# Attention's two banks of a score tile told apart, TensorE's branch hint moved, weight conversions spread again, two penalties on VectorE

## The chip, the cores and the metric

One core of a Trainium2 chip runs the whole program in one launch. The metric is the device time of that core in microseconds (us), lower is better. TensorE (PE) multiplies, ScalarE (ACT), VectorE (DVE) and GpSimd (POOL) work on tiles in SBUF and PSUM, and SyncE (SP) issues most DMAs.

## The reference

Three layers follow one another on 4 x 576 tokens of 512 features.

```python
# attention, 4 batches x 8 heads x 576 x 64
scores = scale * np.matmul(q, k.transpose(0, 1, 3, 2))
kth = np.partition(scores, -32, axis=-1)[..., -32:-31]
scores = np.where(scores >= kth, scores, -1e9)
attn = softmax(scores); out = attn @ v
# experts: each token goes to the one expert of 8 whose normalised embedding is nearest
for e in range(8):
    h = np.maximum(x[mask] @ w1[e], 0.0)
    out[mask] = gate_w[mask, None] * (h @ w2[e])
# last two layers: 512 -> 2048 -> 512
h = x @ w_in
g = np.maximum(h, 0.0) + alpha * np.minimum(h, 0.0)
out = g @ w_out
```

w_in and w_out come as float64, so that each half of one of their units has to be turned from pairs of 32-bit words into floats.

## The kernel before

**Attention.** A tile is 128 queries of a pair of heads; there are nine for each pair and sixteen pairs. Nothing reorders instructions: each engine runs them as the code writes them, and a tile framework adds the waits between engines from the overlaps of what they read and write. The loop `tiles` walks over the tiles with a lag of its own for each stage. For every tile PE makes scores (L189, tile s), ACT copies them (L201, tile ss), DVE finds the 32nd largest (L211 to L224, then L233 and L234 with the help of ACT's sign, L286, and POOL's product, L297), ACT takes exponentials (L291, tile e), and a penalty (tile pen, 1 where a key is to be dropped) is made. The penalty has three makers, and `kind` chooses: 0 is one operation on DVE (L240), 1 one on ACT, 2 three on POOL (nk, mg, pen: L304 to L306). PE transposes e and adds the penalty times minus 2^100 (L322, L323), ACT's Relu brings the result to SBUF (pT, L342, and for the last rows of two tiles pb, L345), and PE multiplies it with the values (L356, L359).

A score tile s is two PSUM banks. When a tile's scores have been copied, their space is lent out: bank 0 holds pt1, the transposed last keys of two tiles, which ACT reads as pb. Bank 1 (`spare_psum`) holds work of the router, which picks the experts and runs between the tiles of the next batch: transposes (L646), dot products (L662, L666) and counts (L716 to L720), read by DVE (tT L653, own L735). The framework orders accesses to one tile, so that pb waits for the router's matmuls written before it, and the router's copies wait for pb.

**Experts.** Nine blocks of tokens go through the experts, two of expert 0 and one for each other, in order of their counts. In a block `blocks` makes eight hidden pieces f (PE; ACT's L1290 and DVE's L1291 evacuate them as hT) and four output pieces dc (y, L1342 and L1344). I number the blocks i = 0 to 8. After each piece `tick` does a share of the block's `plan`: plan[2i] goes with the hidden pieces of block i, plan[2i+1] with its output pieces. An item of a plan is a 512 KB load into one of four buffers raw (SP, L940 or L1000) and, later, its conversion: of an expert's weights one operation each on ACT (L1066) and on DVE or POOL (L1067); a `wide` item, half a unit of w_in or w_out, takes four on DVE (L878, L879, L880, L882) and one on POOL (wf, L1004). Sixteen wide items are dealt out over m entries of the plan from entry `first` on, with `WIDE = (first, m)`. Loads go out three items ahead, and each waits for its buffer.

The width of a block is chosen at run time: `columns_of` writes a piece twice, under a branch on PE. After block 1 one large branch ("narrow") picks one of three written versions of all that follows; a hint for its prefetch stands ahead of it.

**Last layers.** 18 groups k of 256 tokens, nine for each half of the features. For each, PE makes eight features f (L1144 to L1146) and seven products m of group k-1 (L1477, Strassen's scheme), in the order of `MIXED`: f0 f1 1 f2 f3 6 f4 7 f5 5 f6 f7 4 2 3. Each feature or product takes one of six PSUM banks in turn. DVE adds products up (y, L1478), finishes features (L1413) and makes the sums for the scheme (L1434 to L1437); ACT and POOL split operands of products (hT, L1429 and L1430). `weights(k, f)` calls `tick` for the other sixteen wide items in groups 0 to 7; that of (7, 7) converts the last one.

Of the kernel before, what the change touches and what calls it, by code (L numbers as in the profile page):

```python
# [21 lines left out]
P = 128  # L22
# [26 lines left out]
class Attention:  # L49
# [374 lines left out]
    def tiles(self, jobs, first, pair_done, batch_done, drain):  # L424
# [31 lines left out]
        for i in range(-1, n + 9):  # L456
# [6 lines left out]
            self.spare = None  # L463
# [58 lines left out]
class Router:  # L522
# [106 lines left out]
    def pair_done(self, b, hp, mx):  # L629
# [14 lines left out]
        def turn_tail():  # L644
            st["t"] = self.att.spare_psum(P)
            nc.tensor.transpose(st["t"][:D, :P], mx, self.ident)  # L646
        ready = [("wait", lambda: self.routed == b)] if hp == 0 else []
        if b == B - 1 and hp == NPAIR - 1:
# [4 lines left out]
            ("late", lambda: nc.vector.tensor_copy(self.tT[:, hp, :, :TAIL],  # L653
                                                     st["t"][:D, :P].rearrange("p (h t) -> p h t", h=2))),
            lambda: setattr(self, "turned", (b, hp))]

    def dots(self, p, t):

        mm = self.nc.tensor.matmul
# [24 lines left out]
    def batch_done(self, b):  # L684
# [25 lines left out]
        def counts():  # L710
            if b == B - 1:
                p = st["c"] = self.att.ps.tile([P, 4, P], F32, name="pt0", bufs=2).rearrange("p a b -> p (a b)")
            else:
                p = st["c"] = self.att.spare_psum((n + 1) * E)
            for t, (k, _) in enumerate(xs):
                nc.tensor.matmul(p[:, t * E:(t + 1) * E], self.tri[:k], ohb[:k, t], start=True, stop=(t == 0))  # L716
                for u in range(t):
                    nc.tensor.matmul(p[:, t * E:(t + 1) * E], self.ones, ohb[:, u], start=False, stop=(u == t - 1))
            for t, (k, _) in enumerate(xs):
                nc.tensor.matmul(p[:, n * E:(n + 1) * E], self.ones[:k], ohb[:k, t], start=(t == 0), stop=(t == n - 1))  # L720

        def place():
            v.tensor_tensor(off, st["c"][:, :n * E].rearrange("p (a b) -> p a b", b=E), be(self.run), op=OP.add)
            v.tensor_tensor(self.run, self.run, st["c"][:, n * E:(n + 1) * E], op=OP.add)
# [8 lines left out]
        def tile_copy(t):  # L733
            k = xs[t][0]
            v.tensor_copy(lg[:k, t], st[t][:k, k:k + E])  # L735

        def tile_norm(t):
            p, k = st[t], xs[t][0]
            d = wk.tile([P, P], F32, name="diag", bufs=1)
            v.scalar_tensor_tensor(d[:k, :k], p[:k, :k], 1.0, self.ident[:k, :k], op0=OP.mult, op1=OP.mult,  # L740
                                   accum_out=ss[:k, t:t + 1])
# [152 lines left out]
WIDE = (2, 12)  # L894
# [10 lines left out]
class Experts:  # L905
# [271 lines left out]
    def columns_of(self, less, products, whole=False):  # L1177
# [87 lines left out]
    def blocks(self, blocks, plan, which, xT, rows, caps=None):  # L1265
# [7 lines left out]
        for i in which:  # L1273
# [45 lines left out]

            def turn(at):  # L1320
# [4 lines left out]
            for dc in range(4):  # L1325
                if i == 1 and dc == 2:
                    self.tc.mark_branch_hint_location("narrow", "LikelyTaken", ENGINES)
                ps = self.bank()[:, :n]
                for fs in (range(4), range(4, 8)):
# [6 lines left out]
                    self.columns_of(less, products)  # L1336
# [42 lines left out]
    def last_products(self, t, n0, n1):  # L1379
# [158 lines left out]
        for k in range(last + 1):  # L1538
# [3 lines left out]
            for s in order:  # L1542
# [47 lines left out]
                weights(k, f)  # L1590
# [380 lines left out]
```

## Time and profile before

| what | value |
|---|---|
| median of 3 runs (lowest to highest) | 1100.07 us (1098.76 to 1100.5) |
| the profiled execution, its own time | 1102.43 us |
| span of its trace | 1100.6 us |
| PE, DVE, POOL, ACT busy | 96%, 80%, 68%, 66% of the span |
| mean granted clock of PE | 0.992 |

The shares are over the whole span; attention (0 to about 460 us), the experts (to 703.5 us) and the last layers have different bounds, so each is read by itself. An idle time with its releaser (the event that ended it) stands in square brackets in a timeline. Granted clock 1.00 is 2.4 GHz, 0.50 is 1.2 GHz.

### The profile page before, as it was taken

The page shows a single profiled execution, that of the slowest core. Times are in us where ns is not written, and L with a number is a line of the kernel's source. Part 1 is how long each engine was busy: PE and PEld are TensorE (multiplying, and loading weights), DVE is VectorE, ACT ScalarE, POOL GpSimd, SP SyncE. Part 2 cuts the span into 40 slices and gives each one's busy share as a digit, 9 for nine tenths or more (in the row PEclk, how much of TensorE's full clock was granted, in tenths as well). Part 3 has the DMA queues.
Part 4 walks back from the last instruction along what each step waited for, and adds up shares of the span by engine and source line. Part 5 has one row for each costly group of instructions (what it writes and reads, how often), then busy time and mean ns, then how long its engine had stood idle before and what let it go on. Part 6 is the DMA issues. An engine that isn't in the chain of part 4 may idle for free. (4 is left out here: it accounts for less than half of the span.)

```text
span 1100.6 us, 27595 instructions
## 1 busy us (share of the span) xinstructions
PE 1057.3 (96%) x9521; PEld 1004.6 (91%) x9521; DVE 877.0 (80%) x3462; ACT 723.5 (66%) x1546; POOL 745.6 (68%) x788
## 2 busy tenths in 40 slices
PE   5999999999999998999999999999999999999996
PEld 4888889888988897999999999999999999999996
DVE  6999999999999999767676675688899988466555
ACT  6999999999999999735445556454334355433441
POOL 6999999888888888424435544255656685664674
PEclk9999999999999999999999999999999999999998
DMA  7565433343343324267757686137656122212301
GB/s 176 133 154 147 105 96 95 104 124 100 91 109 98 73 65 166 57 206 227 233 195 246 224 268 213 38 96 105 127 119 113 40 63 92 78 58 72 120 22 40
DMA packets 149266, 134.49 MB, mean 122 GB/s; under 512 B 94942, under 2 KB 117470, under 8 KB 149110
## 3 DMA queue, kind: packets, MB, share of 16 engines
q1 hardware_dynamic: 145062, 122.39, 41.0%
q0 software_dynamic: 2912, 9.46, 2.4%
q8 instruction: 85, 1.39, 0.6%
q10 hardware_dynamic: 1136, 0.67, 0.2%
q14 instruction: 71, 0.58, 0.2%
HBM read 89.49 MB, written 33.63 MB: 112 GB/s over the span
## 5 line engine op out<-in xcount | busy, mean ns | idle before, releaser
L1144 PE MATMUL mm<-xT,wt 128*128 128x256 f32 (+7 forms) x852 | 243.1, 285 | 1.6 <-DVE y L1478 1.4
L1145 PE MATMUL mm<-xT,wt 128*128 128x256 f32 (+7 forms) x852 | 243.4, 286 | 0.0
L1146 PE MATMUL mm<-xT,wt 128*128 128x256 f32 (+7 forms) x852 | 242.7, 285 | 0.0
L297 POOL TENSOR_TENSOR sg<-ss,sg 128x576 f32<-128x576 f32 x143 | 201.7, 1413 | 32.3 <-ACT sg L286 30.6
L211 DVE MAX8 cand<-ss 128x8 f32<-128x96 f32 x864 | 210.2, 244 | 8.6 <-ACT ss L201 7.9
L1477 PE MATMUL mm<-wt,hT 128*128 128x256 f32 x1512 | 193.4, 282 | 0.3 <-POOL hT L1430 0.2
L1477 PEld LDWEIGHTS mm<-wt,hT 128*128 128x128 f32 x1512 | 184.9, 189 | 1.2 <-POOL hT L1430 0.6
L1144 PEld LDWEIGHTS mm<-xT,wt 128*128 128x128 f32 x852 | 160.6, 189 | 2.4 <-DVE y L1478 2.1
L1145 PEld LDWEIGHTS mm<-xT,wt 128*128 128x128 f32 x852 | 160.9, 189 | 0.5 <-DVE xT L1375 0.2
L1146 PEld LDWEIGHTS mm<-xT,wt 128*128 128x128 f32 x852 | 160.8, 189 | 0.0
L1004 POOL TENSOR_TENSOR wf<-wa,raw 128x512 f32<-128x512 f32 x32 | 44.9, 1403 | 112.5 <-DVE raw L882 84.2
L286 ACT ACTIVATE sg<-ss,w 128x576 f32<-128x576 f32 x144 | 118.4, 822 | 4.0 <-DVE w L224 3.5
L291 ACT ACTIVATE e<-ss,sm 128x576 f32<-128x576 f32 x144 | 117.7, 817 | 0.0
L322 PE MATMUL pt<-ident,e 128*128 128x128 f32 x576 | 116.3, 282 | 0.3 <-ACT pT L342 0.2
L323 PE MATMUL pt<-away,pen 128*128 128x128 bf16 x576 | 107.4, 222 | 2.7 <-POOL pen L306 2.7
L233 DVE MAX8 w<-sg 128x8 f32<-128x576 f32 x144 | 106.5, 739 | 0.0
L189 PE MATMUL s<-kt,qq 64*128 64x144 f32 (+1 forms) x1280 | 100.9, 311 | 5.2 <-ACT pb L345 2.3
L201 ACT ACTIVATE ss<-s 128x576 f32<-128x576 f32 x144 | 100.2, 696 | 5.4 <-PE s L189 3.4
L1067 POOL TENSOR_TENSOR wt<-raw,wt 128x1024 fp32r<-128x1024 f32 x28 | 70.0, 2502 | 47.7 <-ACT wt L1066 44.8
L189 PEld LDWEIGHTS s<-kt,qq 64*128 64x128 f32 (+1 forms) x1280 | 79.4, 184 | 22.1 <-issue 8.2
L356 PE MATMUL po<-va,pT 128*128 128x65 f32 (+1 forms) x640 | 86.6, 278 | 6.6 <-ACT pc L391 5.9
L342 ACT ACTIVATE pT<-pt 128x512 f32<-128x512 f32 x144 | 91.8, 637 | 1.6 <-PE pt L323 1.6
(301 smaller groups left out, 2729.2 us busy)
## 6 DMA issues: line engine op xcount, KB each, us to landing
raw<-in_moe_w SPq DMA_DIRECT2D x59, 512.0 KB
xr<-yt SPq DMA_DIRECT2D x17, 512.0 KB
qq<-qt SPq DMA_DIRECT2D x60, 144.0 KB
xs<-zeros SPq DMA_DIRECT2D x8, 1028.0 KB
raw<-in_moe_w_in SPq DMA_DIRECT2D x16, 512.0 KB
raw<-in_moe_w_out SPq DMA_DIRECT2D x16, 512.0 KB
yt<-zeros SPq DMA_DIRECT2D x8, 704.0 KB
rows<-in_q SPq DMA_DIRECT2D x32, 144.0 KB
```

Of the source, the lines that this page charges most:

```text
L189: nc.tensor.matmul(s[to, g, c * n:c * n + n], t["qq"][of, h, q0:q0 + m], t["k"][of, h * HALF + c * n:h * HALF + c * n + n], start=True, st ...
L211: blocks.append(lambda i=i: nc.vector.max(A.cand[:, i], A.ss[:, i * BW:(i + 1) * BW if i + 1 < KB else S]))
L233: fin = [lambda: nc.vector.max(C.w[:, 24:32], C.z), lambda: nc.vector.scalar_tensor_tensor(scr, self.vsel, C.c1, C.w[:, 23:32, None].to_br ...
L286: nc.scalar.activation(T.sg, T.ss, AF.Sign, bias=T.w[:, 23:24], scale=-ABOVE, accum_out=T.c1)
L291: nc.scalar.activation(T.e[:, self.place(T)], T.ss, AF.Exp, bias=T.sm[:, 0:1], scale=0.125)
L297: eng.tensor_tensor(T.z, T.ss, T.sg, op=OP.mult)
L322: nc.tensor.matmul(o, T.e[:, k:k + P], self.ident, is_transpose=True, start=True, stop=False)
L323: nc.tensor.matmul(o, T.pen[:, k:k + P], self.away, start=False, stop=True)
L1144: nc.tensor.matmul(ps, wh, xh, start=first, stop=False)
L1145: nc.tensor.matmul(ps, wh, xl, start=False, stop=False)
L1146: nc.tensor.matmul(ps, wl, xh, start=False, stop=last)
L1477: nc.tensor.matmul(ps, a[:, x, c], b[:, y, c], start=c == r == 0, stop=c == 3 and r == 2)
```

## The change

Five edits in one:

1. `kind` returns 0 for the first two tiles: their penalties are made by one operation each on DVE, not by three on POOL.
2. `other_columns` notes the router's accesses to bank 1 of a score tile, and `st_evac_a` declares that ACT's pb (bank 0) does not depend on them, nor they on it. In the last batch (where `tail` is set) nothing changes.
3. PE's hint for "narrow" moves to both sides of a branch one piece of block 1 earlier; that of the other engines stays.
4. `WIDE` goes from (2, 12) to (2, 14): the sixteen wide items lie on plan[2] to plan[15], not plan[2] to plan[13]. By entry they were 1,1,2,1,1,2,1,1,2,1,1,2 and become 1,1,1,1,1,1,2,1,1,1,1,1,1,2. Loads in blocks 2 to 7: before 12, 11, 10, 11, 11, 8; now 11, 10, 11, 10, 10, 11.
5. In `last_products` the weights of (7, 7) are called after products 4, 2 and 3 of that group, not before them.

```diff
     def kind(self, T):
+        if T.n < 2:
+            return 0
...
+    def other_columns(self, x):
+
+        if self.tail is None:
+            if self.piece is not None:
+                self.tc.declare_no_dep(x.ins, self.piece.ins, reason="other columns")
+            self.aside.append(x)
+        return x
...
-            nc.scalar.activation(T.both, T.pt1, AF.Relu)
+            x = nc.scalar.activation(T.both, T.pt1, AF.Relu)
+            if self.tail is None:
+                self.piece = x
+                for a in self.aside:
+                    self.tc.declare_no_dep(x.ins, a.ins, reason="other columns")
...
-            self.spare = None
+            self.spare, self.aside, self.piece = None, [], None
...
-        mm = self.nc.tensor.matmul
+        mm = lambda *a, **k: self.att.other_columns(self.nc.tensor.matmul(*a, **k))
...
-WIDE = (2, 12)
+WIDE = (2, 14)
...
         with self.tc.If(self.room > self.at) as wide:
+            hint()
             products(0)
         with wide.Else():
+            hint()
             products(less)
...
-                    self.tc.mark_branch_hint_location("narrow", "LikelyTaken", ENGINES)
+                    self.tc.mark_branch_hint_location("narrow", "LikelyTaken", ENGINES[1:])
...
-                    self.columns_of(less, products)
+                    self.columns_of(less, products, hint=near if i == 1 and dc == 1 and fs[0] else lambda: None)
...
-                weights(k, f)
+                if (k, f) != (ng - 2, 7):
+                    weights(k, f)
+            if k == ng - 2:
+                weights(k, 7)
```

The same wrapper goes around the router's other matmuls, transposes and copies (L646, L653, L716 to L724, L735, L740).

Three places in the order of the instructions, all on DVE. The first is near the start: ss_125 and ss_129 are the scores of the second and the sixth tile, the row with kth makes the threshold of the second. Before:

```order
L226 TENSOR_TENSOR sm<-w,own 128x4
L234 SCALAR_TENSOR_TENSOR scr,kth<-own,c_318,w 128x18
L600 TENSOR_SCALAR en<-en 8x1
L601 RECIPROCAL en<-en 8x1
L211 MAX cand<-ss_129 128x8
```

And now (the first tile's penalty stands 17 rows earlier, behind the threshold of that tile):

```order
L226 TENSOR_TENSOR sm<-w,own 128x4
L234 SCALAR_TENSOR_TENSOR scr,kth<-own,c_318,w 128x18
L614 TENSOR_SCALAR en<-en 8x1
L615 RECIPROCAL en<-en 8x1
L240 TENSOR_SCALAR pen_133<-ss_125,kth 128x576
L211 MAX cand<-ss_129 128x8
```

One operation over 576 columns has come in ahead of the sixth tile's maxima. The second place is the end of the hidden pieces of block 5 (280 columns wide), on the version of the program that ran. Before:

```order
L1067 TENSOR_TENSOR wt_27248<-raw_9002,wt_27248 128x1024
L1181 UNCONDITIONAL_BRANCH
L1291 SCALAR_TENSOR_TENSOR hT<-mm_8878,hT 128x280
L1291 SCALAR_TENSOR_TENSOR hT<-mm_8877,hT 128x280
L878 TENSOR_SCALAR wa<-raw_9103 128x512
L879 SCALAR_TENSOR_TENSOR wa<-raw_9103,wa 128x512
L880 TENSOR_SCALAR raw_9103<-wa 128x512
L882 SCALAR_TENSOR_TENSOR raw_9103<-raw_9103 128x512
L1291 SCALAR_TENSOR_TENSOR hT<-mm_8874,hT 128x280
L1291 SCALAR_TENSOR_TENSOR hT<-mm_8875,hT 128x280
```

And now:

```order
L1083 TENSOR_TENSOR wt_27263<-raw_8874,wt_27263 128x1024
L1309 SCALAR_TENSOR_TENSOR hT<-mm_8869,hT 128x280
L1309 SCALAR_TENSOR_TENSOR hT<-mm_8866,hT 128x280
L1309 SCALAR_TENSOR_TENSOR hT<-mm_8867,hT 128x280
L1083 TENSOR_TENSOR wt_27356<-raw_9095,wt_27356 128x1024
```

The second wide conversion, four operations, no longer stands ahead of the last two hidden pieces. The third place is the turn from group 7 to group 8 in the last layers: y are the sums of products 4, 2 and 3, the row behind them (L1413) finishes the first feature of group 8. Before:

```order
L1434 TENSOR_TENSOR wt_28682<-wt_28682 128x4x128
L1436 TENSOR_TENSOR wa<-wt_28682 128x512
L1437 TENSOR_TENSOR wt_28682<-wt_28682,wa 128x4x128
L878 TENSOR_SCALAR wa<-raw_8882 128x512
L879 SCALAR_TENSOR_TENSOR wa<-raw_8882,wa 128x512
L880 TENSOR_SCALAR raw_8882<-wa 128x512
L882 SCALAR_TENSOR_TENSOR raw_8882<-raw_8882 128x512
L1478 TENSOR_TENSOR y<-mm_8876,y 128x256
L1478 TENSOR_TENSOR y<-mm_8873,y 128x256
L1478 TENSOR_TENSOR y<-mm_8878,y 128x256
L1413 SCALAR_TENSOR_TENSOR xr_8495<-xr_8495,alpha,mm_8877 128x256
L1022 TENSOR_TENSOR raw_9002<-wf 128x1024
```

And now:

```order
L1458 TENSOR_TENSOR wt_28675<-wt_28675,wa 128x4x128
L1499 TENSOR_TENSOR y<-mm_8868,y 128x256
L1499 TENSOR_TENSOR y<-mm_8865,y 128x256
L1499 TENSOR_TENSOR y<-mm_8870,y 128x256
L894 TENSOR_SCALAR wa<-raw_8874 128x512
L895 SCALAR_TENSOR_TENSOR wa<-raw_8874,wa 128x512
L896 TENSOR_SCALAR raw_8874<-wa 128x512
L898 SCALAR_TENSOR_TENSOR raw_8874<-raw_8874 128x512
L1434 SCALAR_TENSOR_TENSOR xr_8487<-xr_8487,alpha,mm_8869 128x256
L1038 TENSOR_TENSOR raw_8994<-wf 128x1024
```

The three sums now stand ahead of the conversion. On POOL the order at this place is the same before and now: the conversion's wf, then the split hT that reads the sum wa of L1436 and is an operand of product 6.

## Rows read from the trace of the kernel before

**Rows 1.** Attention: length, PE, PEld, DVE, ACT, POOL busy, granted clock, DMA, GB/s.

```profile
40.00:160.00 120.00, 115.08 (x1208) 101.68 (x1206) 112.25 (x723) 119.52 (x269) 112.01 (x143) 1.00 0.46 117
160.00:180.00 20.00, 20.00 (x212) 18.59 (x211) 18.49 (x122) 18.52 (x42) 17.71 (x25) 1.00 0.49 125
```

**Rows 2.** ACT's waits for POOL, 20 to 40 us: total us, times, longest.

```profile
ACT ss L201 <- POOL mg L305: 1.4, 2, 0.8
```

**Rows 3.** DVE's timeline at the start: start, us, instruction, [idle before, releaser].

```profile
22.49 0.14 DVE L600 TENSOR_SCALAR en<-en 8x1 f32<-8x1 f32 x1 [0.60 <-POOL en L599]
...
25.89 0.50 DVE L240 TENSOR_SCALAR pen<-ss,kth 128x576 bf16<-128x576 f32 x1
```

**Rows 4.** ACT's only idle time between 33 and 156 us, from its timeline.

```profile
33.58 0.78 ACT L286 ACTIVATE sg<-ss,w 128x576 f32<-128x576 f32 x1 [0.16 <-DVE w L224]
```

**Rows 5.** ACT's waits before pb over the span: us in total, times, longest.

```profile
ACT pb L345 <- PE s L662: 2.4, 6, 0.5
...
ACT pb L345 <- PE s L666: 2.0, 3, 0.7
...
ACT pb L345 <- PE s L720: 0.7, 3, 0.2
```

**Rows 6.** DVE's timeline late in the router's first stretch.

```profile
189.22 0.28 DVE L653 COPY tT<-s 64x128 f32<-64x128 f32 x1 [0.51 <-ACT pb L345]
```

**Rows 7.** ACT's timeline behind it.

```profile
192.88 0.78 ACT L286 ACTIVATE sg<-ss,w 128x576 f32<-128x576 f32 x1 [0.71 <-DVE w L224]
```

**Rows 8.** PE's timeline, its first idle time after 150 us.

```profile
195.96 1.30 PE L189 MATMUL s<-kt,qq 64*128 64x144 f32 x16 [0.45 <-ACT pb L345]
```

**Rows 9.** PE's timeline, the first instruction behind the "narrow" branch.

```profile
510.40 0.34 PE L1144 MATMUL mm<-xT,wt 128*128 128x400 f32 x1
```

**Rows 10.** The experts' blocks 4 to 8, columns as in Rows 1.

```profile
578.87:606.07 27.20, 27.20 (x206) 27.20 (x205) 17.50 (x26) 14.86 (x25) 14.28 (x8) 1.00 0.72 233
606.07:634.38 28.31, 26.26 (x203) 25.84 (x201) 17.87 (x30) 14.09 (x24) 14.63 (x8) 0.94 0.72 235
634.38:658.44 24.06, 23.53 (x202) 23.04 (x201) 17.82 (x25) 12.54 (x23) 12.20 (x7) 1.00 0.80 264
658.44:681.89 23.45, 23.00 (x202) 22.62 (x201) 12.87 (x24) 14.05 (x25) 13.34 (x6) 1.00 0.82 261
681.89:703.48 21.59, 21.59 (x194) 21.59 (x193) 14.87 (x21) 10.70 (x20) 4.80 (x2) 1.00 0.09 29
```

**Rows 11.** DVE's timeline in block 5's hidden pieces.

```profile
614.27 0.43 DVE L878 TENSOR_SCALAR wa<-raw 128x512 int32<-128x512 int32 x1 [2.75 <-DMA raw<-in_moe_w_out]
...
619.73 0.41 DVE L878 TENSOR_SCALAR wa<-raw 128x512 int32<-128x512 int32 x1
...
621.97 0.80 DVE L1291 SCALAR_TENSOR_TENSOR hT<-mm,hT 128x280 fp32r<-128x280 f32 x2
```

**Rows 12.** PE's timeline at the same place.

```profile
622.47 0.39 PE L1145 MATMUL mm<-hT,wt 128*128 128x264 f32 x1 [1.98 <-DVE hT L1291]
```

**Rows 13.** The stretches behind that wait, columns as in Rows 1.

```profile
622.40:624.40 2.00, 1.93 (x10) 1.93 (x11) 2.00 (x3) 0.38 (x1) 2.00 (x2) 0.64 0.25 86
624.40:626.40 2.00, 2.00 (x11) 2.00 (x11) 1.15 (x4) 1.33 (x2) 2.00 (x1) 0.51 0.72 254
```

**Rows 14.** DVE's timeline at the turn from group 7 to group 8.

```profile
868.35 0.42 DVE L878 TENSOR_SCALAR wa<-raw 128x512 int32<-128x512 int32 x1
...
870.60 1.08 DVE L1478 TENSOR_TENSOR y<-mm,y 128x256 f32<-128x256 f32 x3
```

**Rows 15.** PE's timeline there, feature 2.

```profile
871.07 0.39 PE L1144 MATMUL mm<-xT,wt 128*128 128x256 f32 x1 [1.13 <-DVE y L1478]
```

**Rows 16.** PE's timeline there, product 6.

```profile
874.01 1.84 PE L1477 MATMUL mm<-wt,hT 128*128 128x256 f32 x12
```

**Rows 17.** POOL's timeline there.

```profile
870.77 1.31 POOL L1004 TENSOR_TENSOR wf<-wa,raw 128x512 f32<-128x512 f32 x1 [5.85 <-DVE raw L882]
872.03 2.33 POOL L1430 TENSOR_TENSOR hT<-wa,hT 128x512 fp32r<-128x512 f32 x1
```

More of the change, by code (lines that the diff above doesn't have):

```diff
@@ L645, in turn_tail @@
             st["t"] = self.att.spare_psum(P)
-            nc.tensor.transpose(st["t"][:D, :P], mx, self.ident)
+            self.att.other_columns(nc.tensor.transpose(st["t"][:D, :P], mx, self.ident))
         ready = [("wait", lambda: self.routed == b)] if hp == 0 else []
@@ L652, in pair_done @@
             ("st_sign2", lambda: nc.scalar.activation(self.xT[:, hp, :, :P], st["p"], AF.Copy)),
-            ("late", lambda: nc.vector.tensor_copy(self.tT[:, hp, :, :TAIL],
-                                                     st["t"][:D, :P].rearrange("p (h t) -> p h t", h=2))),
+            ("late", lambda: self.att.other_columns(nc.vector.tensor_copy(
+                self.tT[:, hp, :, :TAIL], st["t"][:D, :P].rearrange("p (h t) -> p h t", h=2)))),
             lambda: setattr(self, "turned", (b, hp))]
     def dots(self, p, t):
-        mm = self.nc.tensor.matmul
+        mm = lambda *a, **k: self.att.other_columns(self.nc.tensor.matmul(*a, **k))
         for c in range(4):
@@ L710, in counts @@
         def counts():
+            mm = lambda *a, **k: self.att.other_columns(nc.tensor.matmul(*a, **k))
             if b == B - 1:
@@ L715, in counts @@
             for t, (k, _) in enumerate(xs):
-                nc.tensor.matmul(p[:, t * E:(t + 1) * E], self.tri[:k], ohb[:k, t], start=True, stop=(t == 0))
+                mm(p[:, t * E:(t + 1) * E], self.tri[:k], ohb[:k, t], start=True, stop=(t == 0))
                 for u in range(t):
-                    nc.tensor.matmul(p[:, t * E:(t + 1) * E], self.ones, ohb[:, u], start=False, stop=(u == t - 1))
+                    mm(p[:, t * E:(t + 1) * E], self.ones, ohb[:, u], start=False, stop=(u == t - 1))
             for t, (k, _) in enumerate(xs):
-                nc.tensor.matmul(p[:, n * E:(n + 1) * E], self.ones[:k], ohb[:k, t], start=(t == 0), stop=(t == n - 1))
+                mm(p[:, n * E:(n + 1) * E], self.ones[:k], ohb[:k, t], start=(t == 0), stop=(t == n - 1))
         def place():
-            v.tensor_tensor(off, st["c"][:, :n * E].rearrange("p (a b) -> p a b", b=E), be(self.run), op=OP.add)
-            v.tensor_tensor(self.run, self.run, st["c"][:, n * E:(n + 1) * E], op=OP.add)
+            free = self.att.other_columns
+            free(v.tensor_tensor(off, st["c"][:, :n * E].rearrange("p (a b) -> p a b", b=E), be(self.run), op=OP.add))
+            free(v.tensor_tensor(self.run, self.run, st["c"][:, n * E:(n + 1) * E], op=OP.add))
         nc.vector.memset(lg[:, 4], 1.0)
@@ L734, in tile_copy @@
             k = xs[t][0]
-            v.tensor_copy(lg[:k, t], st[t][:k, k:k + E])
+            self.att.other_columns(v.tensor_copy(lg[:k, t], st[t][:k, k:k + E]))
         def tile_norm(t):
@@ L739, in tile_norm @@
             d = wk.tile([P, P], F32, name="diag", bufs=1)
-            v.scalar_tensor_tensor(d[:k, :k], p[:k, :k], 1.0, self.ident[:k, :k], op0=OP.mult, op1=OP.mult,
-                                   accum_out=ss[:k, t:t + 1])
+            self.att.other_columns(v.scalar_tensor_tensor(d[:k, :k], p[:k, :k], 1.0, self.ident[:k, :k], op0=OP.mult,
+                                                          op1=OP.mult, accum_out=ss[:k, t:t + 1]))
         def last_copies():
@@ L1175, in bank, with columns_of @@
         return self.mm[(0, 5, 4, 1, 2, 3)[self.used % 6]]
-    def columns_of(self, less, products, whole=False):
+    def columns_of(self, less, products, whole=False, hint=lambda: None):
         if less == 0 or whole:
@@ L1318, in blocks, with near @@
             self.n = len(plan[2 * i + 1])
+            def near():
+                self.tc.mark_branch_hint_location("narrow", "LikelyTaken", ENGINES[:1])
             def turn(at):
```

## The prediction

> **What bounds the kernel now.** I began with the view that gives each engine's busy time by stretch, since the three layers have different limits. In plain attention ACT is busy 119.52 of 120 us and PE 115.08: ACT sets the pace, PE has little to spare. Where the router's dots run, PE is busy 20.00 of 20 and ACT only 18.52: there PE is the one that never rests [rows 1]. In the experts' blocks PE is full in blocks 4 and 8, and lacks 2.05 us in block 5, 0.53 in block 6 and 0.45 in block 7 [rows 10]. In the last layers I looked only for PE's idle time, and the largest is 1.13 us at 871 [rows 15]. After that I read the view of waits and the timelines at each place that an edit touches. An engine that is not the pace-setter of its stretch can gain time without the end moving; this decides most of what follows.
>
> **Edit 1, penalties of the first two tiles.** POOL loses six operations, DVE gets two of about 0.50 us each [rows 3]. What POOL held up was ACT, 1.4 us in two waits behind mg [rows 2], and PE. But the next thing that ACT waits for is DVE, 0.16 us at 33.58, and after that it does not wait until 156 us [rows 4]. So DVE is what is late at 33.58. The first new penalty stands ahead of the row at 22.49, where DVE idles 0.60 us for POOL's en; it fits in there and costs nothing, and without that wait it would cost its 0.50. The second stands behind that row, where DVE has no idle time left before 33.58; it moves DVE, and with it ACT's sign, by 0.50. I take **+0.5**. Bounds: +1.0 if both show, and -1.4 if ACT's freed waits count in full.
>
> **Edit 2, two banks.** ACT's waits for the router's matmuls before pb are 2.4 + 2.0 + 0.7 = 5.1 us over three batches [rows 5]; that is the upper bound of the gain. It can't be had in full: while PE is busy 20.00 of 20 [rows 1], an ACT that passes pb earlier meets PE again at its next operand. What counts is the end of the stretch. There DVE waits 0.51 us at 189.22 for pb before it may read the other bank [rows 6], DVE then is late for ACT's sign by 0.71 at 192.88 [rows 7], and PE, idle for the first time since 150 us, waits 0.45 for pb at 195.96 [rows 8]. Without the tie DVE goes on 0.5 us earlier, and those waits shrink by as much. The other two batches show the same pattern. Three times 0.5 is **-1.5**; bounds 0 (PE's queue keeps all) and -5.1. The router's copies now wait for PE's matmul in place of ACT's pb; nothing stands behind them that PE needs in that stretch earlier than before. In plain attention DVE's wait for pb goes too, and is worth nothing, because ACT has no gap there.
>
> **Edit 3, the hint.** PE goes across the branch into the block of 400 columns at 510.40 with no idle time [rows 9], with the hint at the start of the program. There is nothing to gain: **0**. The Trainium skill ("Runtime: NRT & Kernel Launch", section "Instruction fetch mechanics") says that a taken branch out of the prefetched window has to fetch its target before it goes on. By it a hint that comes nearer would save a stall; this trace shows none, it gives no time for one, and the sum by it would be the same 0 as long as the earlier hint already covers the branch.
>
> **Edit 4, wide conversions.** The lost time of block 5 begins with a load that lands late: DVE stands 2.75 us before a wide conversion at 614.27, then does a second one from 619.73, and only from 621.97 the last two hT [rows 11], for which PE has been idle 1.98 us at 622.47 [rows 12]. Behind it the granted clock is 0.64 and 0.51 for 4 us, mostly the lower of its two levels (1.2 of 2.4 GHz), with 21 matmuls [rows 13]; block 6 runs 202 in its 23.53 busy us, 8.6 a us, so 4 us should hold 34. Thirteen are missing, 1.5 us. Block 5 loses 1.98 + 1.5 = 3.5. The second conversion is what leaves block 5's hidden part; it lasts 621.97 - 619.73 = 2.2 us, more than PE's wait of 1.98, so the wait goes, and the clock's fall with it: -3.5. Block 6 goes from three conversions to two: its 0.53 goes. Block 7 gets three in place of none, the load that block 6 had, at nearly its length (23.45 against 24.06): +0.5. Block 4 now has two in its hidden part, as block 5 had. If a load is as late there, PE's wait is smaller by what the half block is longer: block 5 without its loss is 28.31 - 3.5 = 24.8, half of 27.20 - 24.8 is 1.2, so 1.98 - 1.2 = 0.8. In sum -3.5 - 0.5 + 0.5 + 0.8 = **-2.7**. Bounds: -4.0 (nothing new appears) and +5.7 - 4.0 = +1.7 (the loads of block 7, below). The number of loads up to the end of block 7 stays at 63, and SP issues each only when its buffer is free.
>
> **Edit 5, the last conversion of group 7.** PE waits 1.13 us at 871.07 for the first of three y [rows 15] that stand on DVE from 870.60, behind a conversion that began at 868.35, 2.25 us before [rows 14]. With the y first PE goes on at once, and gains 1.13. But the conversion then ends later by the three y, 1.08 in the row, say 1.0. POOL waits for it (5.85 us before wf at 870.77), and behind wf stands the split of the sum for product 6, done at 872.03 + 2.33 = 874.36 [rows 17]. PE begins product 6 at 874.01 and needs that low half for its third matmul [rows 16]: there is no slack. So the y that PE no longer waits for give way to POOL's hT, which is late next: it ends at 875.4, PE reaches product 6 at about 872.9 and stands there. The end of the group is later by **+1.0**. Bounds: -1.13 (POOL's split is not needed that early) and +2.5: PE's new idle time, 875.4 - 873.1 = 2.3 us, is nearest to the 1.98 behind which the clock fell [rows 12, 13], at 1.5 us more. I leave the clock out of the sum, because only one such fall is shown, and make it a rival. One more thing could lengthen this chain: wf took 1.31 us and hT, of the same shape, 2.33 beside DVE's sums [rows 17]. In the new place both would stand beside them. The Trainium skill ("SBUF — State Buffer", section "SBUF: two separate sides") says that DVE's operations with two SBUF inputs and POOL's exclude each other for their whole length. The two rows agree with it, 1.02 us longer; by the rule wf would be longer too and edit 5 +2.0, the sum -1.7.
>
> **The sum.** 0.5 - 1.5 + 0 - 2.7 + 1.0 = -2.7. On the profiled execution's own 1102.43 it gives 1099.7. That execution lies 2.36 above the median of 1100.07, and since the order of loads is the same in each, I take the sum from the median: **1097.4 us**. A measurement of this kernel can tell about 0.2% (2.2 us) from no change, that is below 1097.9 or above 1102.3.
>
> **Rivals.**
> - *The weights pay.* Product 6 finds its operand in time, because POOL runs the split sooner than I think. Then edit 5 is -1.13 and not +1.0: 1095.3. For it: POOL is idle 5.85 us before wf. Against it: nothing but that conversion ends the idle time.
> - *The banks pay nothing.* PE's 20.00 of 20 holds to the end of the stretch, and the gap at 195.96 only moves. 1098.9.
> - *The clock falls at product 6.* +1.5: 1098.9. For it: the idle time would be longer than the one at 622.47.
> - *Slower: block 7 can't be fed.* It already moves 261 GB/s with eight loads; block 6 has the highest rate of these rows, 264 [rows 10]. Three more loads of 0.524 MB need 1.57 MB / 264 GB/s = 6.0 us of transfers. If they delay DVE's pieces for block 8, which stand behind a conversion that waits, up to 5.7 us appear that the sum does not hold (6.0 less part of the 0.5): 1103.1. It decides when a load of block 7's second half lands after block 7's last y. Against it: block 8 moves only 29 GB/s, so that late loads have room if nothing waits for them.
> - *The start pays.* ACT's 1.4 us are kept: -1.4 in place of +0.5, 1095.5.
>
> **How the numbers follow.** The likeliest, my sum, has 0.36 (its own range is 1096.1 to 1098.7: edit 4 at -4.0, or its new 0.5 and 0.8 twice as large); the weights pay 0.17; the banks pay nothing 0.14; the clock falls 0.13; block 7 can't be fed 0.14; the start pays 0.06. Faster by over 0.2% holds most of the first, and the second and the last: 0.52. Within 0.2%: the third, the fourth and a part of the first: 0.34. Slower: the fifth, 0.14. The range, from 1093 (weights pay, and edit 2 half of its 5.1) to 1102.5 (just short of block 7's full price), leaves out about 0.2.
>
> **What would show it.** Edit 1: PE's wait for pen is gone, and ACT's first sign waits for DVE longer than 0.16 us, or not at all (then I am wrong). Edit 2: no wait of pb for L662 to L720, but PE still full while dots run; the third router stretch ends about 1.5 us earlier, counted from the start of plain attention. Edit 3: no idle time at the branch. Edit 4: block 5 near 24.8 us with clock 1.00, block 6 near 23.5, block 4 up to 28.0. Edit 5: no wait for y at feature 2 of group 8, in its place a wait of product 6 for POOL's hT of about 2.3 us. The prediction fails most easily if a late load falls in block 4 or 7, or if the fall of the clock in block 5 belongs to the profiled execution alone: then the edit has less to give back, and the median gains that much less.

## The result and the profile after

The changed kernel is slower: 1106.46 us median (1103.59 to 1112.84, 8 runs) against 1100.37 us (1098.72 to 1105.39, 8 runs) of the kernel before on the same chip, ratio 1.0061, 95% interval [1.0044, 1.0079]. The prediction said 1097.4 us, in a range up to 1102.5: wrong in size and in direction. The profiled execution took 1106.09 us, with a span of 1104.4 us. The page's first rows of the kernel after show nearly the shares of before (POOL alone has another, 67% for 68%), since the waits in question are short against the span:

```profile
span 1104.4 us, 27604 instructions
PE 1059.9 (96%) x9521; PEld 1008.1 (91%) x9521; DVE 886.8 (80%) x3464; ACT 725.5 (66%) x1546; POOL 742.8 (67%) x782
```

So I cut the span at places that both programs pass: the first eight of ACT's signs, the ends of the router's stretches, the first matmul of each block. Each row is how much longer the profiled execution of after took in that piece; the sum is the difference of the spans, 3.8 us. (The medians are 6.1 apart: the profiled execution of before lay 2.1 above its median, that of after 0.4 below.)

| piece | after minus before, us |
|---|---|
| start, to ACT's eighth sign (33.57, now 36.02) | +2.45 |
| from there to the end of the third router stretch (409.84, now 410.56) | -1.73 |
| end of attention and block 0 (block 1 begins at 486.4, now 488.6) | +1.5 |
| block 1, to the narrow branch (24.05, now 27.77) | +3.72 |
| block 2, behind it (36.38, now 37.84) | +1.46 |
| blocks 3 and 4 | 0.0 |
| blocks 5 to 8 (97.41, now 91.80) | -5.61 |
| last layers (397.1, now 399.1) | +2.0 |

The +1.5 of the fourth row is in part a lower granted clock of PE at the end of attention, 0.50 and 0.82 in the windows from 446 to 450 and to 454 us, against 0.64 and 1.00 before. In e1, e2 and e4 below, which have most of the same edits, the trace gains 0.5 to 0.8 us there against before, so I don't put it down to the change.

**Start.** DVE's timeline of after shows the two new penalties (the first and second row) and a copy behind them:

```profile
19.04 0.52 DVE L240 TENSOR_SCALAR pen<-ss,kth 128x576 bf16<-128x576 f32 x1
...
22.47 1.43 DVE L240 TENSOR_SCALAR pen<-ss,kth 128x576 bf16<-128x576 f32 x1
...
33.02 1.42 DVE L619 COPY tT<-enH 64x64 f32<-64x64 f32 x1
```

and POOL's, at the same two times:

```profile
22.18 1.41 POOL L299 TENSOR_TENSOR sg<-ss,sg 128x576 f32<-128x576 f32 x1
...
32.99 1.40 POOL L299 TENSOR_TENSOR sg<-ss,sg 128x576 f32<-128x576 f32 x1
```

The second penalty takes 1.43 us where another takes 0.50 [rows 3], and the copy, in the trace of before 0.18 us long at 31.81, takes 1.42: each begins just behind the start of a product of POOL (by 0.29 and 0.03 us) and ends just behind its end (by 0.31 and 0.05). The first product comes earlier than before (22.18, before 24.27), since POOL is free of the first two tiles' penalties; the second is met because the copy now comes late (33.02 for 31.81). ACT's timeline shows what it costs:

```profile
25.51 0.77 ACT L288 ACTIVATE sg<-ss,w 128x576 f32<-128x576 f32 x1 [1.84 <-DVE w L224]
28.84 0.78 ACT L288 ACTIVATE sg<-ss,w 128x576 f32<-128x576 f32 x1 [0.79 <-DVE w L224]
...
36.02 0.78 ACT L288 ACTIVATE sg<-ss,w 128x576 f32<-128x576 f32 x1 [1.22 <-DVE w L224]
```

The waits for POOL's mg [rows 2] are gone, as meant, and three waits for DVE, 3.85 us, stand in their place; before, the one at the eighth sign was 0.16 [rows 4]. PE's granted clock is low here, too, 0.50 from 30 to 34 us, but that is not the cause: e13 below, without edit 1, has 0.50 from 18 to 26 us, and its eighth sign at 33.06.

**Router stretches.** ACT's pb waits for no matmul of the router any more [rows 5]. DVE's copy [rows 6] now waits for PE's matmul, as I had said:

```profile
191.37 0.28 DVE L667 COPY tT<-s 64x128 f32<-64x128 f32 x1 [0.52 <-PE s L725]
```

Between 150 and 200 us PE has no idle time; the 0.45 [rows 8] is gone. The next idle time, 0.56 at 200.52, stood in the trace of before as well, at 198.40.

**Narrow branch.** PE's timeline of after, where the block of 400 columns begins [rows 9]:

```profile
512.51 0.27 PE L1162 MATMUL mm<-hT,wt 128*128 128x240 f32 x1
516.35 0.67 PE L1160 MATMUL mm<-xT,wt 128*128 128x400 f32 x1 [3.57 <-issue]
516.82 0.54 PE L1161 MATMUL mm<-xT,wt 128*128 128x400 f32 x1
```

PE stands 3.57 us and, by the word issue, waits for nothing that the profile shows. The view of line 1275, the condition of that branch, names it (durations in ns, PEldq is the sequencer of PE):

```profile
L1275 PEldq COMPARE_BRANCH  x1: 4774/4774/4774, 511.1 to 511.1; - x1
L1275 DVEq COMPARE_BRANCH  x1: 94/94/94, 511.6 to 511.6; - x1
```

In the trace of before the same branch is L1257:

```profile
L1257 PEldq COMPARE_BRANCH  x1: 360/360/360, 508.8 to 508.8; - x1
```

The view of DMA queues of after from 512.5 to 514 us has one transfer on the queue that brings instructions, and that of before from 511 to 512 us, with PE at work, has one, too:

```profile
q8 instruction: 1, 0.02, 3.7%
```

```profile
q8 instruction: 1, 0.02, 6.7%
```

The Trainium skill ("Runtime: NRT & Kernel Launch", section "Instruction fetch mechanics") says that a taken branch to a place that is not yet in the window fetches it first. The 4.77 us agree with that; the Trainium skill gives no price for it. The rows of the queue don't tell the late branch from the one on time, so that the stop is such a fetch is argued here, not shown. Behind the stop the clock is low. Windows, columns as in [rows 1]:

```profile
512.50:516.35 3.85, 0.28 (x3) 0.12 (x2) 0.94 (x1) 0.20 (x1) 0.00 (x0) 0.99 0.90 275
516.35:520.00 3.65, 3.65 (x12) 3.62 (x13) 0.00 (x0) 1.13 (x2) 2.37 (x1) 0.54 0.65 244
520.00:524.00 4.00, 4.00 (x24) 3.89 (x23) 1.15 (x2) 1.94 (x3) 0.00 (x0) 1.00 0.43 135
```

Granted clock 0.54, near the lower level, for 3.65 us loses about 3.65 x 0.46 = 1.7 us, which is near block 2's 1.46.

**Blocks 4 to 8**, in the windows that answer to [rows 10]:

```profile
586.30:613.50 27.20, 27.20 (x206) 27.20 (x206) 20.70 (x30) 15.45 (x25) 13.29 (x8) 1.00 0.72 242
613.50:637.70 24.20, 24.20 (x203) 24.20 (x202) 17.40 (x27) 14.09 (x24) 13.40 (x7) 1.00 0.83 280
637.70:660.60 22.90, 22.90 (x203) 22.90 (x202) 16.80 (x26) 13.95 (x24) 12.92 (x6) 1.00 0.84 269
660.60:683.20 22.60, 22.60 (x202) 22.41 (x201) 17.59 (x25) 12.53 (x23) 13.42 (x7) 1.00 0.81 270
683.20:705.30 22.10, 22.10 (x195) 21.82 (x195) 18.46 (x27) 11.01 (x21) 9.45 (x4) 1.00 0.23 72
```

PE is full and its clock 1.00 in all of them.

**Turn from group 7 to 8.** DVE, POOL and PE in the timelines that answer to [rows 14, 17, 15, 16]:

```profile
870.02 1.08 DVE L1499 TENSOR_TENSOR y<-mm,y 128x256 f32<-128x256 f32 x3
871.02 0.41 DVE L894 TENSOR_SCALAR wa<-raw 128x512 int32<-128x512 int32 x1
```

```profile
873.43 1.32 POOL L1020 TENSOR_TENSOR wf<-wa,raw 128x512 f32<-128x512 f32 x1 [6.83 <-DVE raw L898]
874.71 2.25 POOL L1451 TENSOR_TENSOR hT<-wa,hT 128x512 fp32r<-128x512 f32 x1
```

```profile
877.01 1.58 PE L1498 MATMUL mm<-wt,hT 128*128 128x256 f32 x10 [2.22 <-POOL hT L1451]
```

The wait of 1.13 for y is gone, and product 6 waits 2.22 us for the split. The windows behind it:

```profile
877.00:880.00 3.00, 2.99 (x18) 2.99 (x19) 3.00 (x3) 0.00 (x0) 3.00 (x2) 0.68 0.05 3
880.00:884.00 4.00, 4.00 (x30) 4.00 (x30) 4.00 (x6) 2.46 (x5) 4.00 (x3) 0.81 0.02 4
```

In the trace of before both windows had 1.00.

### The profile page after: what moved, and what is told of

It reads as the page before. It is cut to its first block, busy times and chain, and to the rows that moved or that the text cites. A ratio compares the mean times of both kernels' runs of the same rounds, so it can differ in the third digit from the quotient of the medians.

```text
span 1104.4 us, 27604 instructions
## 1 busy us (share of the span) xinstructions
PE 1059.9 (96%) x9521; PEld 1008.1 (91%) x9521; DVE 886.8 (80%) x3464; ACT 725.5 (66%) x1546; POOL 742.8 (67%) x782
```

## The experiments

"Before" is always the kernel before, on the same chip as the run. Line numbers shift by a few between kernels. The 95% intervals of the ratios reach 1 to 3 us to either side, so the medians alone don't tell e1, e2 and e4 from the changed kernel; what one edit does there is read from the traces.

**e1, edit 3 undone.** The first suspect for the stop at the branch was the hint.

```diff
-  mark_branch_hint_location("narrow", "LikelyTaken", ENGINES[1:])
+  mark_branch_hint_location("narrow", "LikelyTaken", ENGINES)
-  self.columns_of(less, products, hint=near if i == 1 and dc == 1 and fs[0] else lambda: None)
+  self.columns_of(less, products)
```

> The changed kernel with edit 3 alone undone: PE's hint for the narrow branch stands with the others again. Theory (the moved hint no longer covers the branch): PE's 3.57 us without work at the branch and the low clock behind it vanish, some 5 us, so that the time goes from 1106.5 to about 1101.3. Rival (that stop belongs to the one profiled execution, or comes from a page border that the other edits shifted): PE still stands at the branch, and the time stays within 1 us of 1106.5.

Measured: 1105.74 us against 1100.26, 1.0055 [1.0042, 1.0069]; the branch takes 5.59 us. The hint is not the cause, and moving it neither saved nor cost anything that shows. (In the built programs PE's hint stands among the first instructions in before and in e1, and 273 and 247 instructions ahead of the branch, one on either side, in after: so the edit brings it nearer to the branch, where the section on the change has it one piece earlier.)

**e2, edit 1 undone.**

```diff
-        if T.n < 2:
-            return 0
```

> The changed kernel with edit 1 alone undone: POOL makes the first two penalties. Theory (the second penalty on VectorE, 1.43 us beside POOL's product, and what follows on VectorE delays ScalarE's signs): the 2.4 us by which attention is late at its eighth sign vanish, time about 1104. Rival (the delay at the start is given back in attention, where ScalarE sets the pace anyway): within 0.5 us of 1106.5.

Measured: 1104.22 us, 1.0048 [1.0031, 1.0065]. ACT's eighth sign is at 33.06, and the copy takes 0.18 us again. DVE's timeline of this run:

```profile
31.29 0.18 DVE L617 COPY tT<-enH 64x64 f32<-64x64 f32 x1
```

The whole loss of the start goes with edit 1. The branch is still late, 4.64 us.

**e3, edit 4 alone**, in the kernel before.

```diff
-WIDE = (2, 12)
+WIDE = (2, 14)
```

> The kernel before with edit 4 alone, the wide conversions on 14 entries. Theory (blocks 5, 6 and 7 lose their idle time and low clock in every execution): 5 to 6 us faster than before, about 1095. Rival (the loss in block 5 belonged to the profiled execution of the kernel before): 1 to 2 us faster, about 1098.5.

Measured: 1098.10 us against 1100.26, 0.9995 [0.9974, 1.0015]. The twelve times fall into two groups, eight from 1095.26 to 1098.96 and four from 1101.58 to 1105.24; the profiled one, 1096.88, is of the first. Blocks 5 to 8 take 24.23, 22.97, 23.60 and 21.94 us.

**e4, edit 5 undone.**

```diff
-  if (k, f) != (ng - 2, 7):
-      weights(k, f)
-  if k == ng - 2:
-      weights(k, 7)
+  weights(k, f)
```

> The changed kernel with edit 5 alone undone. Theory (the conversion moved behind the sums makes POOL's split for product 6 late by 1.0 us, 2.2 us of waiting in place of 1.1): about 1 us faster than the changed kernel, 1105.4, PE waiting 1.1 us for y at feature 2 of group 8 and hardly for hT. Rival (the moved conversion gains what PE no longer waits for y): about 0.7 us slower, 1107.2.

Measured: 1104.24 us, 1.0044 [1.0028, 1.0060]. The last layers take 397.3 us, with the old wait for y back in PE's timeline:

```profile
873.34 0.39 PE L1160 MATMUL mm<-xT,wt 128*128 128x256 f32 x1 [1.30 <-DVE y L1499]
```

**e5, edit 2 alone**, in the kernel before: all lines of the diff with `other_columns`, `aside` and `piece`, such as

```diff
+                for a in self.aside:
+                    self.tc.declare_no_dep(x.ins, a.ins, reason="other columns")
```

> The kernel before with edit 2 alone. It puts 9 more waiting instructions into PE's program ahead of the narrow branch. Theory (where PE's program stands decides whether the branch's target is there in time, not the hint): PE's compare and branch takes 4 to 6 us in place of 0.36, and the low clock behind it adds 1.5; attention gets 2.2 us shorter; in sum 3 to 4 us slower than before, about 1104. Rival (another edit brings the stop): the branch stays at 0.36 us and the time falls by 2 us to about 1098.

Measured: 1104.44 us against 1099.24, 1.0043 [1.0026, 1.0059]. The branch takes 4.75 us, block 1 27.72 and block 2 38.59, in which PE stands once more, 0.60 us at 517.56, again by issue.

```profile
L1273 PEldq COMPARE_BRANCH  x1: 4747/4747/4747, 507.6 to 507.6; - x1
```

So the edit that was meant for attention is the one that stops PE at a branch 100 us later.

**e6, only instructions.** The built programs differ, ahead of the branch, in the number of instructions on PE: edit 2 adds nine that do nothing but wait. This kernel is the one before with five matmuls of one column at its start, eleven instructions on PE in the built program, and without edit 2.

```diff
+        for _ in range(5):
+            nc.tensor.matmul(self.bank[:, 500:501], ident, ident[:, 0:1], start=True, stop=True)
```

> The kernel before with nothing but five tiny matmuls on PE at the start (one column each, into columns of the PSUM bank own that nothing reads), 11 more instructions ahead of the narrow branch, as many as edits 1 and 2 add. Theory (place of PE's program): compare and branch takes 4 to 6 us, 5 us slower than before. Rival (what the banks edit does to the waits around the branch matters): the branch stays at 0.36 us and the time is that of before.

Measured in a single run: 1113.46 us. The view of the branch's line:

```profile
L1259 PEldq COMPARE_BRANCH  x1: 4721/4721/4721, 514.4 to 514.4; - x1
```

No edit of the change is in this kernel, and the stop is the same. (The matmuls also delay the start: block 1 begins at 491.9 us, so the total says little. In block 2 PE stands once more, 2.25 us at 524.86, by issue.)

**e7, edits 2 and 4 with twelve such matmuls** (`range(12)`), to carry the branch further on, 34 instructions behind its place in before. From here on the expectations count in blocks of 256 instructions; that this length matters no run had shown.

> The kernel before with edits 2 and 4, and twelve tiny matmuls at the start, which put the narrow branch 34 instructions later than before. Theory (place of PE's program, with the branch away from the end of a block of 256 instructions): the branch takes 0.36 us, attention gains 2.2 us and blocks 5 to 7 about 3: 1095. Rival (any later place fails): the branch takes 4 to 6 us and the time is about 1100.

Measured: 1114.53 us against 1099.24, 1.0121 [1.0094, 1.0148], of which the late start is a large part; the branch takes 4.86 us. That place is late too.

**e8, the last conversion still later**, in the kernel before: in group 8, behind the split for product 6.

```diff
+                if (k, f) == (ng - 1, 0):
+                    weights(ng - 2, 7)
...
-                weights(k, f)
+                if (k, f) != (ng - 2, 7):
+                    weights(k, f)
```

> The kernel before with the weights of (7, 7) called in group 8, behind the split for product 6, so that on VectorE the sums y and on GpSimd that split stand ahead of the conversion. Theory (edit 5 fails by GpSimd's order alone): PE waits neither 1.1 us for y at feature 2 of group 8 nor 2.2 us for hT at product 6; 1.0 us faster than before, about 1099.2. Rival (VectorE is full there, so that the wait comes back at the next turn, for y or for a feature): less than 0.3 us of gain.

Measured: 1100.33 us against 1099.24, 1.0002 [0.9982, 1.0022], too wide to rule out the 1.0 us of the theory; the trace decides. In place of one wait of 1.1 us PE has several of 0.2 to 0.7, for y, xT and hT. DVE has no free place there: what stands behind the conversion is late in this trace as well.

**e9 and e10, edits 2 and 4 with 123 and 129 matmuls** spread over the tiles: 255 and 267 instructions more ahead of the branch than before.

```diff
     def st_norm(self, T):
+        if 9 <= T.n < 9 + 123:
+            self.nc.tensor.matmul(self.bank[:32, 500:501], self.away[:, :32], self.away[:, :1], start=True, stop=True)
```

> The kernel before with edits 2 and 4, and one tiny matmul (32 x 1, into columns of the bank own that nothing reads) in each of 123 tiles of attention, which with the 9 waits of edit 2 makes 255 more instructions ahead of the narrow branch: it stands one instruction earlier within a block of 256 than in the kernel before. Theory (the place within the block decides): compare and branch takes 0.36 us, block 1 some 24.0 us and block 2 36.3; with attention 1 to 2 us shorter and blocks 5 to 7 about 3: 1095 to 1097. Rival (any added instruction, or the changed waits, bring the stop): 4.7 us at the branch and 1101 to 1103.

> The same with six more tiny matmuls, 129, so that the branch stands 12 instructions later within its block, where it stands with edit 2 and edit 1. Theory (place within the block): 4.7 us at the compare and branch, 5 to 6 us slower than with 123. Rival (the number of instructions does not matter so finely): the same time as with 123.

The view of the branch's line, e9 and then e10:

```profile
L1275 PEldq COMPARE_BRANCH  x1: 339/339/339, 530.1 to 530.1; - x1
```

```profile
L1275 PEldq COMPARE_BRANCH  x1: 5021/5021/5021, 533.0 to 533.0; - x1
```

The branch is on time with 255 more and late with 267: twelve instructions decide between 0.34 and 5.02 us. The totals, 1122.09 us (1.0182 [1.0156, 1.0207]) and 1130.01, tell nothing more: the added matmuls cost attention about 20 us, since PE has little to spare there.

**e11, edit 1 for the first tile only**, in the kernel before.

```diff
+        if T.n < 1:
+            return 0
```

> The kernel before with edit 1 for the first tile alone. Theory (the first penalty lies in VectorE's idle time and only the second one, 1.43 us beside GpSimd's product, is late): 0 to 1 us faster than before, 1099 to 1100. Rival (every penalty moved to VectorE delays ScalarE's signs): half of edit 1's loss, 1 us slower, 1101.

Measured: 1102.19 us against 1100.76, 1.0011 [0.9995, 1.0027]. The penalty that met POOL's product is gone; the copy still meets one, 1.42 us at 31.58, and ACT's eighth sign waits 1.91 for DVE, at 34.59: about 1 us lost in place of 2.45.

**e12 to e14, the branch carried on by code that never runs.** Edits 2 and 4, and ahead of block 1 a branch that is never entered around 121, 40 or 80 matmuls.

```diff
+            if i == 1:
+                with self.tc.If(self.room > 2000):
+                    for _ in range(40):
+                        nc.tensor.matmul(self.mm[0][:, :1], self.ident, self.ident[:, :1], start=True, stop=True)
```

> The kernel before with edits 2 and 4, and a branch on PE ahead of block 1 whose body (121 tiny matmuls) is never run: it only moves the narrow branch by 255 instructions in all, one instruction earlier within its block of 256 than in the kernel before. Theory (the place within the block decides, and edits 2 and 4 are gains in themselves): the narrow branch takes 0.36 us, no work is added to attention, and the time is 3 to 5 us below that of before, 1096 to 1098. Rival (edit 2 gains nothing, or the skipped body costs a fetch of its own): within 1 us of before, or a compare and branch of over 2 us ahead of block 1.

> The kernel before with edits 2 and 4 and a skipped body of 40 tiny matmuls ahead of block 1: the narrow branch stands 93 instructions later than in the kernel before, near place 70 of its block of 256. If a fetch is late only when the branch stands close to the end of a block: compare and branch 0.36 us, and the shorter skip costs less than the 3.5 us of the long one; time 1096 to 1098. If the place of the kernel before is one of few that work: 4.7 us at the branch and about 1103.

> The same with 80 skipped matmuls, place 150 of the block. If only places close to the end of a block or behind its start are late: 0.36 us at the narrow branch. If the place of the kernel before is one of few that work: 4.7 us. The skip itself, over 161 instructions, should cost between nothing and 3.5 us.

e12: 1102.56 us against 1100.88, 1.0023 [1.0002, 1.0044]. The narrow branch takes 0.34, but the new one over 121 matmuls takes 3.52; PE stands as long at the start of block 1. e13: 1099.08 against 1099.85, 0.9995 [0.9981, 1.0010]; narrow 0.76, the new one 0.49, block 1 23.95, block 2 36.20. e14, a single run: 1105.41; narrow 4.54, block 1 27.41.

In e13 block 8 takes 27.18 us in place of 21.6 [rows 10]. DVE's timeline of e13, conversions of expert weights and hidden pieces of block 8:

```profile
680.41 2.74 DVE L1081 TENSOR_TENSOR wt<-raw,wt 128x1024 fp32r<-128x1024 f32 x1 [2.11 <-ACT wt L1080]
...
683.71 3.17 DVE L1081 TENSOR_TENSOR wt<-wf,wt 128x1024 fp32r<-128x1024 f32 x1
...
688.06 3.32 DVE L1081 TENSOR_TENSOR wt<-wf,wt 128x1024 fp32r<-128x1024 f32 x1
691.31 0.71 DVE L1311 SCALAR_TENSOR_TENSOR hT<-mm,hT 128x240 fp32r<-128x240 f32 x2
```

POOL's, with conversions of the same form:

```profile
683.39 2.40 POOL L1081 TENSOR_TENSOR wt<-wf,wt 128x1024 fp32r<-128x1024 f32 x1 [1.32 <-ACT wt L1080]
687.92 2.38 POOL L1081 TENSOR_TENSOR wt<-wf,wt 128x1024 fp32r<-128x1024 f32 x1 [2.12 <-ACT wt L1080]
```

and PE's:

```profile
691.75 0.38 PE L1159 MATMUL mm<-hT,wt 128*128 128x240 f32 x1 [2.11 <-DVE hT L1311]
```

In e3, where block 8 takes 21.94, the first such pair is, on DVE and on POOL:

```profile
684.02 1.21 DVE L1067 TENSOR_TENSOR wt<-wf,wt 128x1024 fp32r<-128x1024 f32 x1
```

```profile
684.11 3.39 POOL L1067 TENSOR_TENSOR wt<-wf,wt 128x1024 fp32r<-128x1024 f32 x1 [1.73 <-PE mm L1146]
```

The engine that begins first keeps its length, and the other's conversion lasts longer: in e13 POOL begins 0.32 us ahead, and DVE takes 3.17 us in place of 1.21; in e3 DVE begins 0.09 ahead, and POOL takes 3.39 in place of 2.40. DVE's conversions stand ahead of block 8's hidden pieces, so PE waits for them where POOL was first, 3.2 us in all in e13. Of the eleven traces with edit 4, POOL begins first in four (e1, e9, e13, e14, by 0.04 to 0.32 us), with a block 8 of 25.44 to 27.18 us, and DVE in seven (by 0.09 to 0.62), with 21.94 to 22.44; in the six without it these conversions don't meet, and none is over 21.62. It is not a load that comes late: DVE waits for ACT's half of the conversion ahead of these 2.1 to 2.4 us in the four and 2.5 to 3.0 in the seven. What decides which engine is first stays open.

**e15, edit 2 alone with the 40 matmuls that never run**, the place of e13.

> The kernel before with edit 2 (the two banks told apart) and 40 matmuls that are never run, written under a branch ahead of block 1, so that the narrow branch stands at the place where it was not late with edits 2 and 4. If edit 2's gain in attention (about 0.7 us in each of three batches) is real and its only cost was the place of the narrow branch, this kernel ends about 2 us earlier than the kernel before: ratio 0.998, with block 1 near 24 us, block 2 near 36.3 and no stall of block 8 (that one came with edit 4). If the gain of attention is given back later, at the router's end or in the blocks, the ratio is 1.000.

Measured: 1098.91 us against 1099.61, 0.9994 [0.9983, 1.0005]. Block 1 takes 23.94 us, block 2 36.18, and the branch is on time with edit 2 in place:

```profile
L1273 PEldq COMPARE_BRANCH  x1: 438/438/438, 507.5 to 507.5; - x1
```

The gain that attention shows, 1.5 us, is less than the measurement can tell; 0.45 us of it goes again at the branch around the 40 matmuls, where PE waits, and a block 6 of 27.31 us in the profiled execution (PE waits 2.3 us for hT, clock 0.94) is as large as the gain. No version that I found is faster than the kernel before by more than its interval.

**The place of the branch.** Counted in the built programs, the number of PE's instructions ahead of the narrow branch, against the time of the branch:

| instructions more than in before | kernels | branch, us |
|---|---|---|
| 0 and 1 | before, e3, e8; e11 | 0.36 |
| 9 to 12 | e5, e2, e1, e6, e4, after | 4.64 to 5.59 |
| 34 | e7 | 4.86 |
| 93 | e13, e15 | 0.76, 0.44 |
| 173 | e14 | 4.54 |
| 255 | e9, e12 | 0.34 |
| 267 | e10 | 5.02 |

The place decides in every pair that I could make. By what rule stays open: that 255 is on time like 0, and 267 late like 11, fits a count modulo 256, but no run tests another length, and between 9 and 173 late and on time alternate in no order that the rows explain. The branch also moves together with its target and the code behind it, so the runs don't tell whose place it is.

## Why the prediction was wrong

**Edit 3 and edit 2, the step that failed.** The prediction priced the branch at 0 with "this trace shows none", and edit 2 by its waits alone. The row that I read [rows 9] was true of the kernel before. That none of the edits would alter what it shows was an assumption, and it stood unspoken: edit 2 puts nine more instructions on PE ahead of the branch, edit 1 two and edit 3 one. Nine suffice (e5), eleven that have nothing to do with the change do the same (e6), and putting the branch elsewhere takes the stop away with edit 2 in place (e9, e13, e15). Its price is 3.7 us in block 1 and 1.5 (after) to 2.7 us (e7) in block 2, by the low clock behind it and in e5 also by the second stop of 0.60; in e6, where that one takes 2.25, it is 5.2. No rival of mine had it; even the section of the Trainium skill that I cited spoke of such a stall, and I used it for the hint's place only. The hint itself is worth nothing here, as predicted, but in a kernel that does stop (e1).

**Edit 2, its gain.** Predicted -1.5, measured -1.73 in after and -1.5 in e15 from the eighth sign to the end of the third stretch. The traces with it have 374.5 to 375.6 us there, those without 376.3 to 376.9 (e6, e7, e9 and e10, with matmuls added in this piece or before, apart). Mechanism and size were right.

**Edit 1.** Predicted +0.5, measured +2.45 in after (2.2 in e4, 0.9 in e1). The mechanism "DVE is late at 33.58" was right. In e1 the penalty meets POOL's product as well (1.44 us), but the copy begins at 32.27, ahead of the product at 32.85, and takes 0.65; the loss is smaller by that. The term is mis-sized because I took a penalty's 0.50 from a place with no product of POOL beside it. The rule that I used for edit 5 speaks of this one too: the Trainium skill ("SBUF — State Buffer", section "SBUF: two separate sides") says that some DVE operations and POOL's exclude each other for their whole length, and lower on that page that copies and operations with a scalar can be among them. The rows agree: 0.50 became 1.43, 0.18 became 1.42.

**Edit 4.** Predicted -2.7. In after, blocks 4 to 8 gain 5.6 us, but against a block 5 of 28.31 us that belonged to the profiled execution in part: without edit 4, block 5 took 25.5 to 26.3 us in e5, e6, e8, e11 and e15. That is the case that the end of the prediction names, in part: the edit had less to give back. Against these, e3's block 5 is better by some 1.8, and its block 6 by 1.5 (24.2 to 24.8, without e15's 27.31). Block 4 lost nothing of the 0.8 that I had put there. The rest is a loss of 3.8 to 5.6 us in block 8, in some executions only (4 of 11 traces). My rival "block 7 can't be fed" named its place, DVE's pieces for block 8 behind a conversion, and its size, but the size by luck: it is not loads that come late but POOL's conversion that begins before DVE's. The two together could give e3's two groups of times and its ratio near 1. That the slow group of e3 is this stall was not seen in a trace of e3 itself.

**Edit 5.** The chain came out step by step: the wait for y gone, POOL's split ending at about 877, product 6 waiting 2.22 us where I had said 2.3. And the rival's clock came with it in after and e1, 0.68 and 0.81 in after's two windows behind, but not in e2, where product 6 waits 2.48 us. The last layers take 398.6 to 399.1 us with edit 5 (e2, e1, after) and 396.7 to 398.1 in the others, e7's 405.0 apart: about +1.7, not +1.0. The split took 2.25 us in its new place and wf 1.32, so wf did not get longer: it began at 873.43, ahead of DVE's conversion L1038 at 873.66, which took 2.17 us in place of 1.22. That conversion, not the sums of DVE, is also what the split stood beside in the trace of before (L1022, 871.99 to 873.21).

**The sum.** With the sizes that the runs showed: +2.2 (edit 1), -1.5 (edit 2), +3.7 and +2 (the branch), -3.0 in most executions and +2 in the others (edit 4), +1.7 (edit 5), together +5.1 where block 8 doesn't stall and +10 where it does; measured +6.1 in the medians.

## What to carry to other kernels

A row "no idle time here" prices a place only as long as the edit leaves that place's surroundings alone: ahead of a large run-time branch, every instruction added to the engine that takes it, waits too, can move the cost of the branch, so look at the branch's own row after any change, however far away. A duration taken for a moved operation must come from a row with the same neighbour on the other engine; here POOL's product beside it made DVE's operation last three to eight times as long. And one profiled execution may hold a loss that the next doesn't have: of block 5's 4.1 us that the edit gave back, about two were of this kind, and block 8's stall hangs on which of two engines begins first, by 0.04 to 0.62 us.

## What the runs showed of the hardware

- The same branch of PE, over the same code, took 0.34 to 0.76 us or 4.5 to 5.6 us, by the number of instructions ahead of it (e6, and e9 against e10). Also a branch over 121 matmuls that never ran took 3.52 us, over 40 0.40 and 0.49, over 80 0.40.
- DVE's operations of one input, a penalty (0.50 us alone) and a copy of 64 x 64 (0.18), took 1.43 and 1.42 us where POOL's product had begun 0.29 and 0.03 us before them, and ended 0.31 and 0.05 behind it. Of two conversions of one form (128x1024, two inputs) on DVE and POOL, the one that began first took 1.21 (DVE, e3) or 2.40 us (POOL, e13), the other 3.39 (POOL) or 3.17 (DVE).
- After 2.2 us (product 6) and 3.6 us (the branch) without work PE's granted clock was 0.68 and 0.54 in the next 3 to 4 us; after the 1.30 us of e4 and the 2.48 us of e2 (product 6) it stayed at 1.00, in the windows behind those waits, e4's and e2's:

```profile
873.30:877.00 3.70, 3.66 (x28) 3.47 (x29) 3.70 (x6) 1.69 (x5) 3.70 (x3) 1.00 0.39 109
```

```profile
873.00:876.00 3.00, 2.07 (x17) 2.07 (x18) 3.00 (x4) 0.00 (x0) 3.00 (x2) 1.00 0.04 3
876.00:880.00 4.00, 4.00 (x36) 4.00 (x35) 4.00 (x5) 2.39 (x6) 4.00 (x3) 1.00 0.02 4
```
